# The second feed-forward product of three batches by seven half products instead of eight

## The chip, the cores and the metric

The kernel runs on one core of a Trainium2 chip. Its time is the device time of one execution in microseconds (us), given as the median of several runs. The profiled execution is a run of its own. The engines are called TensorE (PE in the profile; PEld is its weight load), VectorE (DVE), ScalarE (ACT), GpSimd (POOL) and SyncE (SP), which issues most of the DMAs.

## What is computed

Attention in which a query sees only keys of its own cluster, for 4 batches of 8 heads with 768 tokens of 64 values, and behind it a feed-forward network (FFN) over 3072 tokens: a product with `w_in` (512 x 2048), a gate on each element, and a product with `w_out` (2048 x 512). The change concerns the FFN.

```python
q_assign = np.argmax(np.einsum('bhsd,hcd->bhsc', q_n, c_n), axis=-1)
k_assign = np.argmax(np.einsum('bhsd,hcd->bhsc', k_n, c_n), axis=-1)
mask = q_assign[:, :, :, None] == k_assign[:, :, None, :]
scores = np.where(mask, scale * np.matmul(q, k.transpose(0, 1, 3, 2)), -1000000000.0)
attn = np.exp(scores - np.max(scores, axis=-1, keepdims=True))
attn = attn / (np.sum(attn, axis=-1, keepdims=True) + 1e-09)
x = np.matmul(attn, v).transpose(0, 2, 1, 3).reshape(B * S, H * D)
h = x @ w_in
g = h * np.clip(h + 3.0, 0.0, 6.0) / 6.0
out = g @ w_out
```

## The kernel before

The attention runs over 16 pairs of heads, four pairs to a batch. A pair has 12 steps `n`, so there are 192 in all: two halves of 384 queries by six blocks of 128 keys. The main loop takes two steps at a time. An iteration issues, in this order, the scores of two steps (`scores`, matmul L354, exp L366 on ScalarE), the products with the values of the two steps before (`attn_v`, L383), at the end of a half the division by the sums (`divide`: matmul `pd` L404, reciprocal L408, multiply L409 into `xT`), and then items of the FFN (`fill`) in turn with steps that prepare the next pair (`prep_items`: transposes L278, cluster scores L291, routing L302 to L334). The running sums of the exponentials are added up by GpSimd (L370, L373). In the first half of the loop it also loads and decodes 32 chunks of weights (`decode_weights`, L208 to L231, on ScalarE and VectorE). The order is written out by hand; every engine takes its instructions in that order.

`ffn_items(b)` makes 56 items for a batch, 28 for each half of 384 tokens. An up item multiplies 4 blocks of 128 rows of `w_in_sb` with `xT` (L434, output 128x384), and gates the result: ScalarE writes `t` = relu(h/6 + 0.5) (L441), VectorE writes `gT` = min(t, 1) * h (L443). `gT` has 17 buffers, `t` has 2. A down item (L456) multiplies 4 of 16 gated blocks with 512 columns of `w_out_sb`; four items fill one PSUM bank `py` with 128 tokens, VectorE copies it to `y` (L462) and SyncE stores it (L463). `ph` and `py` share the two banks of the pool `psum_m`. All operands are float32.

How many items an iteration takes is set by `items_by(n)`: 16 while weights are still being decoded (up to step DECODED = 96), the other 40 of batch 0 by step END = 104, and from there 56 items in 48 steps. A batch's items are added when its last division has been issued. The items of the last batch, and what is left of the one before, run behind the loop with no attention beside them.

## Time and profile before

| | |
|---|---|
| median of 3 runs | 1141.31 us (1139.34 to 1145.62) |
| profiled execution, its own time | 1144.7 us |
| its span in the profile | 1142.7 us |
| TensorE busy | 1081.2 us (95%), 4402 instructions |
| VectorE busy | 408.4 us (36%), 499 instructions |
| ScalarE busy | 380.2 us (33%), 740 instructions |
| GpSimd busy | 300.5 us (26%), 187 instructions |

The span is what the profiler recorded on the core; the execution's own time holds 2.0 us more around it. Busy shares are means over the whole span, so a stage has to be read from a view by stretch. Records of matmuls overlap one another, since an end is modelled: what a matmul costs in a row of matmuls is read from start to start.

### The profile page before, as it was taken

The page shows a single profiled execution, that of the slowest core. Times are in us where ns is not written, and L with a number is a line of the kernel's source. Part 1 is how long each engine was busy: PE and PEld are TensorE (multiplying, and loading weights), DVE is VectorE, ACT ScalarE, POOL GpSimd, SP SyncE. Part 2 cuts the span into 40 slices and gives each one's busy share as a digit, 9 for nine tenths or more (in the row PEclk, how much of TensorE's full clock was granted, in tenths as well). Part 3 has the DMA queues.
Part 4 walks back from the last instruction along what each step waited for, and adds up shares of the span by engine and source line. Part 5 has one row for each costly group of instructions (what it writes and reads, how often), then busy time and mean ns, then how long its engine had stood idle before and what let it go on. Part 6 is the DMA issues. An engine that isn't in the chain of part 4 may idle for free.

```text
span 1142.7 us, 11066 instructions
## 1 busy us (share of the span) xinstructions
PE 1081.2 (95%) x4402; PEld 520.0 (46%) x4402; DVE 408.4 (36%) x499; ACT 380.2 (33%) x740; POOL 300.5 (26%) x187
## 2 busy tenths in 40 slices
PE   6987797999899999999999999999999999999996
PEld 3433343444444544554445544454445544544542
DVE  5799896788711120231122301222112211210210
ACT  4665574675411310333223322333124310200200
POOL 3755554544401100233222313223122320000000
PEclk8988898999999999999999999999999999999999
DMA  5233333342302000020020102020010000000000
GB/s 128 77 85 91 97 84 88 97 106 65 78 10 61 1 6 22 1 42 1 13 57 1 42 9 51 10 42 1 10 33 1 1 10 18 1 9 19 1 9 22
DMA packets 83532, 42.77 MB, mean 37 GB/s; under 512 B 76304, under 2 KB 76304, under 8 KB 83472
## 3 DMA queue, kind: packets, MB, share of 16 engines
q1 hardware_dynamic: 83328, 41.95, 14.4%
q8 instruction: 36, 0.59, 0.2%
q14 instruction: 24, 0.20, 0.1%
q10 hardware_dynamic: 144, 0.03, 0.0%
HBM read 35.68 MB, written 6.29 MB: 37 GB/s over the span
## 4 chain that ended last, share of the span: by engine, by line
PE 82%; DVE 17%; issue 0%; ACT 0%; POOL 0%; DVEq 0%; POOLq 0%
PE py L456 29%; PE ph L434 28%; PE ps L354 11%; PE pv L383 8%; DVE rcp L408 3%; DVE one_hot L322 2%; DVE wunit L228 2%; DVE wtop L221 2%; PE pqk L278 2%; DVE wtop L217 1%; DVE wunit L224 1%; DVE w_in_sb L231 1%; PE pd L404 1%; DVE xT L409 1%; PE pcs L291 1%; DVE tie L312 1%
## 5 line engine op out<-in xcount | busy, mean ns | idle before, releaser
L434 PE MATMUL ph<-xT,w_in_sb 128*128 128x384 f32 x1024 | 347.3, 491 | 3.2 <-DVE gT L443 3.2
L373 POOL TENSOR_TENSOR acc<-acc,ex 128x768 f32<-128x768 f32 x128 | 238.4, 1862 | 424.0 <-ACT ex L366 418.8
L456 PE MATMUL py<-w_out_sb,gT 128*128 128x512 f32 x768 | 338.7, 595 | 0.0
L434 PEld LDWEIGHTS ph<-xT,w_in_sb 128*128 128x128 f32 x1024 | 188.9, 190 | 148.3 <-issue 21.5
L456 PEld LDWEIGHTS py<-w_out_sb,gT 128*128 128x128 f32 x768 | 142.8, 190 | 176.4 <-issue 174.8
L366 ACT ACTIVATE ex<-ps 128x768 f32<-128x768 f32 x192 | 150.5, 806 | 183.4 <-PE ps L354 183.2
L441 ACT ACTIVATE t<-ph,half_c 128x384 f32<-128x384 f32 x128 | 74.3, 581 | 363.7 <-PE ph L434 363.7
L354 PE MATMUL ps<-xf 64*128 64x384 f32 x768 | 175.4, 536 | 3.1 <-ACT ex L366 3.0
L443 DVE SCALAR_TENSOR_TENSOR gT<-t,ph 128x384 f32<-128x384 f32 x128 | 70.8, 553 | 298.4 <-ACT t L441 298.4
L383 PE MATMUL pv<-ex,vt 128*64 128x384 f32 x768 | 146.5, 503 | 0.0
L462 DVE COPY y<-py 128x512 f32<-128x512 f32 x24 | 16.6, 691 | 286.6 <-PE py L456 286.6
L370 POOL TENSOR_TENSOR acc<-ex 128x768 f32<-128x768 f32 x32 | 59.4, 1857 | 202.1 <-ACT ex L366 202.1
L408 DVE RECIPROCAL rcp<-pd 128x384 f32<-128x384 f32 x32 | 81.7, 2554 | 68.2 <-PE pd L404 68.1
L354 PEld LDWEIGHTS ps<-xf 64*128 64x128 f32 x768 | 67.0, 197 | 62.2 <-issue 41.1
L383 PEld LDWEIGHTS pv<-ex,vt 128*64 128x64 f32 x768 | 46.9, 137 | 83.7 <-issue 78.0
L354 PE MATMUL ps<-xm 64*128 64x384 bf16 x384 | 65.7, 337 | 0.7 <-ACT xm L338 0.7
L280 ACT COPY xf<-pqk 128x384 f32<-128x384 f32 x64 | 29.1, 481 | 69.2 <-PE pqk L278 69.2
L338 ACT CAST xm<-po 128x512 bf16<-128x512 f32 x48 | 27.4, 581 | 41.9 <-PE po L334 41.9
L228 DVE SCALAR_TENSOR_TENSOR wunit<-raw,wunit 128x512 f32<-128x512 uint32 x32 | 35.6, 1112 | 1.1
L278 PEld LDWEIGHTS pqk<-ident,qk 128*128 128x128 f32 x192 | 24.2, 149 | 22.1 <-issue 13.8
L354 PEld LDWEIGHTS <-xm 64*128 64x128 bf16 x384 | 19.9, 98 | 27.7 <-issue 4.1
L334 PEld LDWEIGHTS <-one_hot 128*128 128x128 bf16 x192 | 13.7, 101 | 41.4 <-issue 23.1
(70 smaller groups left out, 466.0 us busy)
## 6 DMA issues: line engine op xcount, KB each, us to landing
raw<-in_moe_w_in_dram SPq DMA_DIRECT2D x16, 512.0 KB, 3.7
raw<-in_moe_w_out_dram SPq DMA_DIRECT2D x16, 512.0 KB, 3.6
qk<-in_q_dram SPq DMA_DIRECT2D x32, 192.0 KB, 3.8
qk<-in_k_dram SPq DMA_DIRECT2D x32, 192.0 KB, 4.2
vt<-in_v_dram SPq DMA_DIRECT2D x32, 192.0 KB, 4.2
out_dram<-y SPq DMA_DIRECT2D x24, 256.0 KB, 2.0
cen<-in_centroids_dram ACTq DMA_DIRECT2D x1, 32.0 KB, 1.7
```

The lines of the kernel that those rows point to most:

```text
L228: nc.vector.scalar_tensor_tensor(out=unit, in0=lo, scalar=2.0**-52, in1=unit, op0=ALU.mult, op1=ALU.mult)
L278: nc.tensor.transpose(out=pt[:, i], in_=qk[:, j // NCH, j % NCH], identity=ident)
L354: nc.tensor.matmul(st["ps", n][:, t, 0:HALF], lhsT=x[r, NCH + j], rhs=x[r, hf * NHC : (hf + 1) * NHC], start=first, stop=not first,)
L366: nc.scalar.activation(out=ex, in_=sc, func=ACT.Exp, scale=SM_SCALE)
L370: nc.gpsimd.tensor_tensor(out=acc, in0=st["ex", n - 1], in1=ex, op=ALU.add)
L373: nc.gpsimd.tensor_tensor(out=acc, in0=acc, in1=ex, op=ALU.add)
L383: nc.tensor.matmul(pv[t * D : (t + 1) * D], lhsT=vt[:, j, t], rhs=ex[:, t], start=(j == 0), stop=(j == NCH - 1),)
L408: nc.vector.reciprocal(out=rcp, in_=pd)
L434: nc.tensor.matmul(hh, lhsT=w_in_sb[:, kt, f * P : (f + 1) * P], rhs=xT[:, kt, hf * HALF : (hf + 1) * HALF], start=(kt == 0), stop=(kt == ...
L441: nc.scalar.activation(out=t, in_=hh, func=ACT.Relu, bias=half_c, scale=1.0 / 6.0)
L443: nc.vector.scalar_tensor_tensor(out=gT, in0=t, scalar=1.0, in1=hh, op0=ALU.min, op1=ALU.mult)
L456: nc.tensor.matmul(py, lhsT=st["g", f][:, i * P : (i + 1) * P], rhs=w_out_sb[:, f], start=(f == 0), stop=(f == NFT - 1),)
```

## The change

For batches 1 to 3 `fast_items` takes the place of `ffn_items`. It makes 45 items for a batch: three blocks of 256 tokens, each with 8 up items and 7 down items. An up item multiplies 256 tokens with two blocks of `w_in_sb`, one from the first half of the 2048 hidden values and one from the second, into one PSUM bank (L504, eight matmuls of 256 columns), and gates the whole bank (`gate`, L427 and L428) into four places of `g_sb`. Every second up item adds four VectorE sums of 128x256 (L516), which make three further operands (kinds 4 to 6) and change kind 1 in place. A down item is one of seven products (L522, eight matmuls of 256 columns), which go to the halves of two banks X and Y; ScalarE copies (L547) and VectorE adds (L529) combine them into `y0` and `y1`, 128 tokens each, which SyncE stores.

The weights that these products need are three new tiles T1, T2 and T4 and one quarter of `w_out_sb` that is changed in place (T3). `weight_sums` makes them with eight VectorE subtractions of 128x1024 (L493), one in each iteration from step 96 to step 110. T1, T2 and T4 take the memory of the decoding buffers, which are closed there. Batch 0 keeps `ffn_items`, now with the gate in place in 18 slots of `g_sb`. To make room, `smallp` and `nump` have one buffer instead of two, and `in_range` writes over `rcp` instead of into tiles of its own. `items_by` paces 45 items over 48 steps from END on.

```diff
@@ -128,16 +128,15 @@
-    smallp = pool("smallp", 2)
+    smallp = pool("smallp", 1)
 ...
-    nump = pool("nump", 2)
+    nump = pool("nump", 1)
 ...
-    tp = pool("tp", 2)
-    gp = pool("gp", NFT + 1)
-    yp = pool("yp", 2)
-    rawp = pool("rawp", 2)
-    decp = pool("decp", 2)
+    yp = pool("yp", 1)
+    decoding = ctx.enter_context(ExitStack())
+    rawp = decoding.enter_context(tc.tile_pool(name="rawp", bufs=2))
+    decp = decoding.enter_context(tc.tile_pool(name="decp", bufs=2))
 ...
+    g_sb = const.tile([P, 7, NFT // 2, P], F32, name="g_sb")
 ...
     def in_range(i, rcp):
-        same = nump.tile([P, HALF], BF16, name="same", tag="same")
-        nc.scalar.activation(out=same, in_=rcp, func=ACT.Copy, accum_out=totals[:, 0, i : i + 1])
-        lack = nump.tile([P, HALF], BF16, name="lack", tag="same")
+        nc.scalar.activation(out=rcp, in_=rcp, func=ACT.Copy, accum_out=totals[:, 0, i : i + 1])
         nc.scalar.activation(
-            out=lack, in_=rcp, func=ACT.Relu, bias=low_c, scale=-1.0, accum_out=totals[:, 1, i : i + 1]
+            out=rcp, in_=rcp, func=ACT.Relu, bias=low_c, scale=-1.0, accum_out=totals[:, 1, i : i + 1]
         )
 ...
+    def gate(g, h):
+        nc.scalar.activation(out=g, in_=h, func=ACT.Relu, bias=half_c, scale=1.0 / 6.0)
+        nc.vector.scalar_tensor_tensor(out=g, in0=g, scalar=1.0, in1=h, op0=ALU.min, op1=ALU.mult)
     def ffn_items(b):
+        slots = g_sb.rearrange("p k i c -> p (k i c)")
 ...
-                t = tp.tile([P, HALF], F32, name="t")
-                nc.scalar.activation(out=t, in_=hh, func=ACT.Relu, bias=half_c, scale=1.0 / 6.0)
-                gT = gp.tile([P, HALF], F32, name="gT")
-                nc.vector.scalar_tensor_tensor(
-                    out=gT, in0=t, scalar=1.0, in1=hh, op0=ALU.min, op1=ALU.mult
-                )
-                st["g", f] = gT
+                at = (hf * NFT + f) % 18 * HALF
+                st["g", f] = slots[:, at : at + HALF]
+                gate(st["g", f], hh)
 ...
                 if part == 3:
-                    y = yp.tile([P, DM], F32, name="y")
+                    y = yp.tile([P, DM], F32, name="y", tag=f"y{i % 2}")
                     nc.vector.tensor_copy(out=y, in_=py)
                     nc.sync.dma_start(out_v[b, hf * NHC + i], y)
 ...
+        return items
+    HF, HC = NFT // 2, DM // 2
+    wb = [[w_out_sb[:, t * HF : (t + 1) * HF, c * HC : (c + 1) * HC] for c in range(2)] for t in range(2)]
+    def weight_sums(i):
+        if i == 0:
+            decoding.close()
+            wtp = pool("wtp", 1)
+            for name in ("T1", "T2", "T4"):
+                st[name] = wtp.tile([P, HF, HC], F32, name=name)
+            st["T3"] = wb[0][1]
+        name, a, b = (
+            ("T1", wb[0][1], wb[0][0]), ("T2", wb[1][1], st["T1"]), ("T4", wb[1][0], st.get("T2")),
+            ("T3", wb[1][1], wb[0][1]),
+        )[i // 2]
+        h = slice(i % 2 * HF // 2, (i % 2 + 1) * HF // 2)
+        nc.vector.tensor_tensor(out=st[name][:, h], in0=a[:, h], in1=b[:, h], op=ALU.subtract)
+    def fast_items(b):
+        def up(m, i):
+            def item():
+                xT = st["xT", b]
+                ph = psum_m.tile([P, 512], F32, name="ph", tag="m")
+                for t in range(2):
+                    f = t * HF + i
+                    for kt in range(NKT):
+                        nc.tensor.matmul(
+                            ph[:, t * HC : (t + 1) * HC], lhsT=w_in_sb[:, kt, f * P : (f + 1) * P],
+                            rhs=xT[:, kt, 2 * m * P : 2 * (m + 1) * P],
+                            start=(kt == 0), stop=(kt == NKT - 1),
+                        )
+                gate(g_sb[:, 0:4, i], ph.rearrange("p (k c) -> p k c", k=4))
+                if i % 2:
+                    a11, a21, a12, a22, s1, s2, s4 = (g_sb[:, k, i - 1 : i + 1] for k in range(7))
+                    for out_, in0, in1, op in (
+                        (s1, a21, a22, ALU.add), (s2, s1, a11, ALU.subtract),
+                        (a21, a11, a21, ALU.subtract), (s4, a12, s2, ALU.subtract),
+                    ):
+                        nc.vector.tensor_tensor(out=out_, in0=in0, in1=in1, op=op)
+            return item
+        def product(bank, half, kind, w, first, last, again):
+            for i in range(HF):
+                nc.tensor.matmul(
+                    bank[:, half * HC : (half + 1) * HC], lhsT=g_sb[:, kind, i], rhs=w[:, i],
+                    start=(first and i == 0), stop=(last and i == HF - 1),
+                    skip_group_check=again,
+                )
+        def add(out_, in0, in1):
+            nc.vector.tensor_tensor(out=out_, in0=in0, in1=in1, op=ALU.add)
+        def down(m, part):
+            def item():
+                if part == 0:
+                    st["X"] = psum_m.tile([P, DM], F32, name="X", tag="m")
+                    st["y0"] = yp.tile([P, DM], F32, name="y0", tag="y0")
+                elif part == 2:
+                    st["Y"] = psum_m.tile([P, DM], F32, name="Y", tag="m")
+                    st["y1"] = yp.tile([P, DM], F32, name="y1", tag="y1")
+                kind, bank, half, w = (
+                    (0, "X", 0, wb[0][0]), (5, "X", 1, st["T2"]),
+                    (4, "Y", 0, st["T1"]), (1, "Y", 1, st["T3"]),
+                    (2, "X", 0, wb[1][0]), (6, "Y", 0, wb[1][1]), (3, "Y", 1, st["T4"]),
+                )[part]
+                product(st[bank], half, kind, w, part in (0, 2), part in (1, 3, 4, 6), part > 3)
+                y0, y1 = st["y0"], st.get("y1")
+                if part == 1:
+                    nc.scalar.copy(out=y0[:, HC:], in_=st["X"][:, HC:])
+                    add(y0[:, HC:], y0[:, HC:], st["X"][:, 0:HC])
+                elif part == 3:
+                    add(y1[:, 0:HC], y0[:, HC:], st["Y"][:, HC:])
+                    add(y1[:, HC:], y1[:, 0:HC], st["Y"][:, 0:HC])
+                elif part == 4:
+                    nc.scalar.copy(out=y0[:, 0:HC], in_=st["X"][:, 0:HC])
+                elif part == 6:
+                    add(y1[:, 0:HC], y0[:, HC:], st["Y"][:, HC:])
+                    nc.sync.dma_start(out_v[b, 2 * m + 1], y1)
+                    add(y0[:, HC:], y0[:, HC:], st["Y"][:, 0:HC])
+                    nc.sync.dma_start(out_v[b, 2 * m], y0)
+            return item
+        items = []
+        for m in range(NHC):
+            items += [up(m, i) for i in range(HF)] + [down(m, part) for part in range(7)]
 ...
+    per_fast = NHC * (HF + 7)
 ...
-        return per_ffn + (n - END) * per_ffn // per_batch
+        return per_ffn + (n - END) * per_fast // per_batch
 ...
             if m >= 0 and m % per_batch == per_batch - 1:
-                fill += ffn_items(m // per_batch)
+                fill += (fast_items if m >= per_batch else ffn_items)(m // per_batch)
 ...
+            if n >= DECODED and (n - DECODED) // 2 < 8:
+                weight_sums((n - DECODED) // 2)
```

The places of the program that the prediction speaks of, as the built programs have them. First TensorE, the last FFN, which runs behind the loop; `ph` is the up product, `py`, `X` and `Y` are the banks of the down products, `T_2515`, `T_2514` and `T_2516` are T2, T1 and T4. Before:

```order
L404 MATMUL pd<-acc,ones 64x384 x2
L434 MATMUL ph<-xT,w_in_sb 128x384 x64
L456 MATMUL py<-w_out_sb,gT 128x512 x48
L434 MATMUL ph<-xT,w_in_sb 128x384 x64
L456 MATMUL py<-w_out_sb,gT 128x512 x48
```

After, its last block of 256 tokens:

```order
L504 MATMUL ph<-xT,w_in_sb 128x256 x64
L522 MATMUL X<-w_out_sb,g_sb 128x256 x8
L522 MATMUL X<-T_2515,g_sb 128x256 x8
L522 MATMUL Y<-T_2514,g_sb 128x256 x8
L522 MATMUL Y<-w_out_sb,g_sb 128x256 x8
L522 MATMUL X<-w_out_sb,g_sb 128x256 x8
L522 MATMUL Y<-w_out_sb,g_sb 128x256 x8
L522 MATMUL Y<-T_2516,g_sb 128x256 x8
```

Two rounds of 64 and 48 matmuls of 384 and 512 columns have become three rounds of 64 and 56 matmuls of 256 columns.

Second VectorE at the end of a block in the same FFN. Before, behind 16 gates, the three copies of a half and the gates of the next:

```order
L409 TENSOR_TENSOR xT<-num,rcp 128x384
L443 SCALAR_TENSOR_TENSOR gT<-t,ph 128x384 x16
L462 COPY y<-py 128x512 x3
L443 SCALAR_TENSOR_TENSOR gT<-t,ph 128x384 x16
L583 TENSOR_SCALAR good<-totals 128x32 x2
```

After, the last two gates of a block, their sums, the adds of its products (`y_5612` is y0, `y_5632` is y1) and the first gates of the next:

```order
L428 SCALAR_TENSOR_TENSOR g_sb<-g_sb,ph 128x4x128 x2
L516 TENSOR_TENSOR g_sb<-g_sb 128x256 x4
L529 TENSOR_TENSOR y_5612<-y_5612,X 128x256
L529 TENSOR_TENSOR y_5632<-y_5612,Y 128x256
L529 TENSOR_TENSOR y_5632<-y_5632,Y 128x256
L529 TENSOR_TENSOR y_5632<-y_5612,Y 128x256
L529 TENSOR_TENSOR y_5612<-y_5612,Y 128x256
L428 SCALAR_TENSOR_TENSOR g_sb<-g_sb,ph 128x4x128 x2
```

Four sums now stand in VectorE's queue between a pair of gates and what follows, and five adds where copies stood.

Third VectorE behind the decoding of the last chunk of weights, about steps 94 to 100. Before:

```order
L231 TENSOR_TENSOR w_out_sb<-wtop,wunit 128x512
L462 COPY y<-py 128x512 x2
L408 RECIPROCAL rcp<-pd 128x384
L409 TENSOR_TENSOR xT<-num,rcp 128x384
L462 COPY y<-py 128x512
L443 SCALAR_TENSOR_TENSOR gT<-t,ph 128x384 x16
L306 TENSOR_REDUCE mx<-pr 128x24
```

After:

```order
L231 TENSOR_TENSOR w_out_sb<-wtop,wunit 128x512
L463 COPY y<-py 128x512 x2
L493 TENSOR_TENSOR T_2514<-w_out_sb 128x1024
L408 RECIPROCAL rcp<-pd 128x384
L409 TENSOR_TENSOR xT<-num,rcp 128x384
L463 COPY y<-py 128x512
L428 SCALAR_TENSOR_TENSOR g_sb<-g_sb,ph 128x384 x8
L493 TENSOR_TENSOR T_2514<-w_out_sb 128x1024
L428 SCALAR_TENSOR_TENSOR g_sb<-g_sb,ph 128x384 x8
L493 TENSOR_TENSOR T_2515<-w_out_sb,T_2514 128x1024
L306 TENSOR_REDUCE mx<-pr 128x24
```

The first weight sums stand ahead of a division and among the gates of batch 0; the other five follow in the same way, one in each iteration.

## Rows read from the trace of the kernel before

**Rows 1.** The page: busy time of TensorE; its granted clock in 40 slices.

```profile
PE 1081.2 (95%) x4402; PEld 520.0 (46%) x4402; DVE 408.4 (36%) x499; ACT 380.2 (33%) x740; POOL 300.5 (26%) x187
...
PEclk8988898999999999999999999999999999999999
```

**Rows 2.** Busy time by stretch (us from the span's start), with granted clock.

```profile
core 0: us, PE busy (x) PEld busy (x) DVE busy (x) ACT busy (x) POOL busy (x), PEclk, DMA share, GB/s
...
280.00:320.00 40.00, 34.52 (x171) 16.63 (x170) 28.89 (x37) 21.05 (x46) 17.22 (x10) 0.96 0.25 65
320.00:360.00 40.00, 40.00 (x116) 17.91 (x115) 4.50 (x4) 2.88 (x5) 3.62 (x2) 1.00 0.03 13
...
590.00:724.00 134.00, 134.00 (x557) 63.63 (x553) 28.93 (x39) 42.20 (x76) 37.11 (x21) 1.00 0.10 24
...
968.00:1134.00 166.00, 165.84 (x453) 85.13 (x449) 25.72 (x45) 19.66 (x36) 0.00 (x0) 1.00 0.03 10
```

**Rows 3.** The chain that ended last: shares; then pieces by start, duration, what.

```profile
PE 82%; DVE 17%; issue 0%; ACT 0%; POOL 0%; DVEq 0%; POOLq 0%
...
302.49 2.48 DVE rcp L408
...
316.61 3.63 PE py L456 x8
320.24 0.33 PE pqk L278 x3
320.56 3.44 PE py L456 x8
...
1010.05 41.20 PE py L456 x96
1051.25 41.28 PE ph L434 x128
```

**Rows 4.** The page's groups: busy, mean ns, idle time before, releaser.

```profile
L434 PE MATMUL ph<-xT,w_in_sb 128*128 128x384 f32 x1024 | 347.3, 491 | 3.2 <-DVE gT L443 3.2
...
L456 PE MATMUL py<-w_out_sb,gT 128*128 128x512 f32 x768 | 338.7, 595 | 0.0
```

**Rows 5.** Timeline behind the last up pass: start, duration, engine, line, operation.

```profile
1092.37 7.89 PE L456 MATMUL py<-w_out_sb,gT 128*128 128x512 f32 x18
1092.57 0.58 ACT L441 ACTIVATE t<-ph,half_c 128x384 f32<-128x384 f32 x1 [2.00 <-PE ph L434]
...
1093.18 0.56 DVE L443 SCALAR_TENSOR_TENSOR gT<-t,ph 128x384 f32<-128x384 f32 x1 [2.03 <-ACT t L441]
1093.23 0.19 PEld L456 LDWEIGHTS py<-w_out_sb,gT 128*128 128x128 f32 x1 [0.24 <-issue]
```

**Rows 6.** Timeline of TensorE between two iterations.

```profile
643.20 5.33 PE L434 MATMUL ph<-xT,w_in_sb 128*128 128x384 f32 x16
648.46 0.92 PE L354 MATMUL ps<-xf 64*128 64x384 f32 x4
...
652.36 2.85 PE L434 MATMUL ph<-xT,w_in_sb 128*128 128x384 f32 x8
```

**Rows 7.** Line 302 from 330 to 960 us: weight loads, ns min/median/max.

```profile
L302 PEld LDWEIGHTS pr<-ident,cs x21: 139/141/143, 422.1 to 846.0; 128*128 128x128 f32 x21
```

**Rows 8.** VectorE, lines 409 and 231 before 320 us, 409 from 330: min/median/max.

```profile
L409 DVE TENSOR_TENSOR xT<-num,rcp x15: 557/950/2135, 43.1 to 305.0; 128x384 f32<-128x384 f32 x15
...
L231 DVE TENSOR_TENSOR w_in_sb<-wtop,wunit x16: 691/692/2182, 19.4 to 178.0; 128x512 f32<-128x512 f32 x16
...
L409 DVE TENSOR_TENSOR xT<-num,rcp x16: 557/558/558, 358.4 to 918.8; 128x384 f32<-128x384 f32 x16
```

**Rows 9.** Timeline behind the last down pass.

```profile
1133.57 0.27 PE L592 MATMUL pl<-ident,one 128*1 128x128 f32 x1
1133.77 0.69 DVE L462 COPY y<-py 128x512 f32<-128x512 f32 x1 [13.04 <-PE py L456]
...
1134.49 0.33 SPq L463 DMA_DIRECT2D out_dram<-y  x1
```

## The prediction

> **What bounds the kernel now.** I read the busy times by engine and the granted clock first [rows 1]: TensorE is busy for 1081.2 us of a span of 1142.7, and after the first slices the granted clock stays at 90% or more of 2.4 GHz. The busy times by stretch [rows 2] say where that share is an average over two stages. Up to about 320 us VectorE is the late engine (28.89 us of the 40 before 320, with TensorE at 34.52 and its clock once below full); from 320 us to the last matmul TensorE is busy in every microsecond at a granted clock of 1.00 (134 of 134, and 165.84 of 166 in the last stretch), VectorE for at most 22% of the time. The chain that ended last [rows 3] agrees: until about 305 us it runs through VectorE's reciprocals and weight decoding, and from then on through TensorE, 82% of the span in all. Everything that the change replaces runs after that point. So the question is how many TensorE microseconds it removes, and whether it makes TensorE wait. Today TensorE waits for the gate twice, 3.2 us in all [rows 4].
>
> The unit of the sum is one **pass**. A float32 matmul appears in the trace as two matmul records: the program has 512 up products and 384 down products, the trace 1024 and 768 [rows 4]. In the last feed-forward network (FFN) nothing lies between them, and there the chain gives clean prices [rows 3]: 128 up passes of 384 columns in 41.28 us are 322.5 ns each, 96 down passes of 512 columns in 41.20 us are 429.2 ns each. Three 128-column transposes, also float32 with 128x128 weights, take 0.33 us in the same view, 110 ns each.
>
> **The change part by part.** *Up product.* Per batch, 32 items of 4 matmuls at 384 columns become 24 items of 8 matmuls at 256: 256 passes become 384, with the same number of columns in all. No pass of 256 columns is in the trace, but it lies between two that are. The slope from 384 to 512 columns is 106.7 ns per 128 columns, and from 128 to 384 it is (322.5-110)/2 = 106.3; so 256 columns should cost 322.5-106.7 = 215.8 ns. The neighbours bound it: it can't be below 110 nor, if its weights arrive in time, above 322.5. I take 215.8, since both slopes agree. Before: 256 x 322.5 ns = 82.56 us. After: 384 x 215.8 ns = 82.87 us. It loses 0.3 us per batch.
>
> *Down product.* Per batch, 96 matmuls of 512 columns (192 passes) become 3 blocks x 7 products x 8 matmuls of 256 columns (336 passes): 192 x 429.2 ns = 82.40 us against 336 x 215.8 ns = 72.51 us. It gains 9.89 us per batch. The seven-for-eight ratio alone would give 10.3; the rest goes to the small constant in each of the extra passes. Both together are 9.6 us per batch and **28.7 us for batches 1 to 3**, all of it on the bounding engine. If the pass price were off by 1 ns, the 2160 new passes would move this by 2.2 us.
>
> *Changes of shape on TensorE.* A run of FFN passes that follows an attention product starts dearer: the first 8 down passes behind one take 3.63 us, 8 behind a transpose 3.44 [rows 3], and a run that ends before the scores costs 0.1 us more (5.26 us from start to start for 16 up passes, against 5.16 at 322.5 ns) [rows 6]. The order has 66 such entries in both programs, and 61 exits (runs or transposes before the scores or the sums over values) in both. I cost them at nothing.
>
> *The gate in place and in blocks.* It now covers 128x512 once per 16 passes (3.45 us) where it covered 128x384 per 8 passes (2.58 us). ScalarE's part takes 0.58 us and VectorE's 0.56 us now, and the gate ends 1.37 us after the last up pass has handed over to the next [rows 5]. With 512 columns both steps grow by a third at most, 0.19 us each, to 0.77 and 0.75 us: 1.75 us. Who waits for it: the eighth matmul of a block's first product, which starts 14 passes or 3.0 us later. That leaves 1.25 us. A PSUM buffer comes free 1.75 us after its item, and the other buffer's item gives 3.45 us of cover. Cost nothing; without that cover, at most 1.75 us per item.
>
> *Sums of gated blocks (L516).* Four VectorE sums of 128x256 behind every second gate, 144 in all. The nearest rows are a 128x384 multiply at 557 ns and a 128x512 sum at 691 [rows 8]; one step of 128 columns further down gives 0.42 us each, 1.7 us a pair. Held up by a GpSimd instruction one could cost 1.5 us more (the 128x512 sum takes from 691 to 2182 ns while the weights are decoded). VectorE's need per pair is 2 x 0.75 + 1.7 = 3.2 us against 6.9 us of passes. Queued behind them are the next gate, the reciprocals and the routing steps, and for the first two sums a block's second product, whose seventh matmul starts 6.0 us after the last up pass; the two sums that it needs end by 1.75 + 0.85 = 2.6 us. Cost nothing.
>
> One thing speaks against that cover. In the trace, all 16 late multiplies with two SBUF inputs took 557 to 558 ns, though GpSimd is busy for 37.11 of 134 us in those stretches; early ones went up to 2135 [rows 8, 2]. The Trainium skill, "SBUF — State Buffer", section "Who interferes with whom", says that a VectorE instruction with two SBUF inputs contends with a GpSimd instruction that reads SBUF. The early rows agree. By it the new sums would meet GpSimd's adds, which the old gate with its one SBUF input did not, and two held up in a pair make 6.2 us of the 3.2; by the late rows the pair stays at 3.2. Either is under 6.9 us, so it is a matter for the second rival's chance and not for the sum.
>
> *Adds of products and output.* Five adds and two ScalarE copies per block replace two copies of 0.69 us [rows 9]: about 2.1 us of VectorE for 1.4, beside passes. Part 4 writes bank X again two products (6.9 us) after its readers could start, part 5 writes Y again one product (3.45 us) after. At the very end it is open: today one copy and one store follow the last pass; then two adds and two stores. Between -0.3 us (one add of half the width gates the first store) and +1.0 (a full add and an issue of 0.33 us more), I take **+0.5 us**.
>
> *Weight sums.* Eight VectorE sums of 128x1024, about 1.2 us each by the same slope, issued over iterations 96 to 110 behind the gates of each iteration, where VectorE is nearly idle (4.50 of 40 us) [rows 2]. The first is needed several items later. Nothing. The loads of q, k, v share SP's queue with the stores; their number stays, and they are issued a pair ahead. Single buffers for num, rcp and the small tiles: a new num or rcp comes six steps of the loop after the last, and its readers take four of them. Nothing, or a few tenths in the early stage.
>
> Sum against the profiled execution: 1144.7 - 28.7 + 0.5 = 1116.5 us. It lies 3.4 us above the median of the runs, 1141.31, inside their spread (1139.34 to 1145.62). Against the median: **1113.1 us**.
>
> **The rivals.** *First: weights that don't arrive in time.* The load of 128 columns is recorded with 190 ns, the new pass gives it 216. If the load couldn't lie beside the pass before it, each of the 2160 passes would cost some 110 ns more (the transpose's whole price, load included): 238 us, 1351 us, slower. The point where it decides is 229.1 ns a pass: 720 such passes cost what a batch's FFN costs now (165.0 us). Only 13 ns separate it from my price. Against it: the transpose's load is recorded with 141 ns [rows 7] and yet transposes follow each other at 110, so the record is longer than the time for which a load holds anything; and loads lie wholly inside the passes before them at 384 and 512 columns [rows 5]. The Trainium skill, "TensorE: Matmul & The Clock Gate", section "The mechanism" in Part 3, says that a weight load overlaps with matmuls in flight only where the row groups differ, which 128-row weights don't. By that rule this rival would come true; the trace disagrees, with 429.2 ns from pass to pass and the 190 ns inside. Chance 0.04.
>
> *Second: a gate that comes late.* If the sums wait for GpSimd, or stand before a gate behind a reciprocal (2.48 us) and its multiply (0.56), TensorE waits at a block's first product or for a PSUM buffer. For it: VectorE gets some 22 us more per batch, 144 sums and wider adds. Against it: VectorE is busy 28.93 of 134 us, and the scores and sums of an iteration put 3.90 us of TensorE work between its last item and the next one's first [rows 6]. Two microseconds at each of 9 blocks are 18 us: about 1131 us; half of that, 1122. Only from 3.2 us a block would it eat the gain. Chance 0.10.
>
> *Third: another engine becomes the bound.* VectorE would need to go from 28.93 to 129 us per half batch, ScalarE from 42.20; neither does. That the products don't become narrower can be excluded: the order shows 504 of 256 columns in place of 288 of 512. Chance 0.02, counted with the gain within 0.5%.
>
> **How the numbers follow.** Forecast 0.84, at 1113.1, itself good to about 1108 to 1118 (1 ns a pass, the end, the runs' spread of -2 and +4). Second rival 0.10, first 0.04, third 0.02. The range goes up to half of the second rival's cost and down to a pass 2 ns cheaper: 1107 to 1123. About 0.5%, or 5.7 us, is what a measurement of this kernel can tell from no change; so faster 0.94 (forecast and nearly all of the second), same 0.02, slower 0.04.
>
> **What would show it.** From start to start, passes of L504 and L522 at 216 ns, and the last FFN in 155.4 us where it took 165.2: that is the sum. TensorE busy in the whole of every stretch behind 320 us, no wait for g_sb over 0.3 us a block: the cover holds. VectorE's share there up from 22% to about 30%: the sums cost it but not the time. I am wrong if a pass takes over 218 ns, if TensorE has gaps before X, or if the early stage, which the change hardly touches, ends later than 320 us.

## The result and the profile after

The changed kernel takes 1109.34 us (median of 4 runs, 1108.17 to 1109.79), against 1143.12 us (1139.34 to 1145.62) for the kernel before beside it: a ratio of 0.971, with an interval of 0.967 to 0.974. The forecast was 1113.1 us, with a range of 1107 to 1123. The profiled execution took 1108.17 us, with a span of 1106.3.

The page of the changed kernel, against [rows 1, 3, 4]: TensorE does 32 us less, VectorE 58 us more.

```profile
PE 1049.0 (95%) x5218; PEld 674.7 (61%) x5218; DVE 466.6 (42%) x654; ACT 385.0 (35%) x734; POOL 301.3 (27%) x187
...
PEclk8999998999899999999999999999999999999999
...
PE 82%; DVE 15%; issue 1%; ACT 1%; POOL 0%; DVEq 0%; POOLq 0%
...
L504 PE MATMUL ph<-xT,w_in_sb 128*128 128x256 f32 x1152 | 259.6, 382 | 0.0
```

The chain that ended last, with start, duration and work of each piece, against [rows 3]: the last reciprocal of the early stage (the 15th), and the last FFN.

```profile
291.22 2.48 DVE rcp L408
...
994.13 27.63 PE ph L504 x128
1021.75 6.91 PE X L522 x32
1028.66 6.91 PE Y L522 x32
1035.57 3.45 PE X L522 x16
1039.02 6.91 PE Y L522 x32
1045.93 27.63 PE ph L504 x128
```

128 up passes in 27.63 us are 215.9 ns each, 32 down passes in 6.91 us the same. But the reciprocal that stood at 302.49 us now stands at 291.22, in a stage in which no FFN item has changed but the place of its gate.

Busy time by stretch, against [rows 2]:

```profile
core 0: us, PE busy (x) PEld busy (x) DVE busy (x) ACT busy (x) POOL busy (x), PEclk, DMA share, GB/s
280.00:320.00 40.00, 34.39 (x138) 16.50 (x137) 17.91 (x26) 13.21 (x27) 10.38 (x6) 0.91 0.11 24
320.00:360.00 40.00, 40.00 (x120) 18.86 (x119) 7.44 (x8) 3.74 (x6) 3.62 (x2) 1.00 0.20 49
400.00:500.00 100.00, 98.97 (x420) 56.64 (x419) 28.63 (x43) 23.90 (x41) 18.92 (x11) 1.00 0.08 20
600.00:700.00 100.00, 100.00 (x536) 70.45 (x535) 28.54 (x47) 32.28 (x57) 27.23 (x15) 1.00 0.13 30
700.00:800.00 100.00, 98.15 (x532) 67.23 (x530) 28.20 (x47) 34.20 (x59) 28.72 (x16) 1.00 0.11 27
```

VectorE stands at 28 to 29%, far from full. TensorE is no longer busy in every microsecond: it lacks 1.03 us in one stretch of 100 and 1.85 in another. What it waited for behind 300 us (total, times, longest; the kernel before has no such wait behind 310 us):

```profile
PE po L334 <- ACT xm L338: 2.1, 2, 1.0
PE pqk L278 <- ACT xf L280: 1.6, 2, 0.8
```

So the span of 1142.7 us became 1106.3 by three differences. I cut both traces at the start of the 16th reciprocal (TensorE is the late engine from there on) and at TensorE's last record:

| us | before | after | difference | forecast |
|---|---|---|---|---|
| to the 16th reciprocal | 355.74 | 344.68 | -11.1 | 0 |
| from there to TensorE's last record | 777.83 | 752.88 | -24.9 | -28.7 |
| from there to the end of the span | 9.16 | 8.72 | -0.4 | +0.5 |

The middle one falls apart again. Summed over all FFN passes from their starts to the next start on TensorE, the work of the FFN is 29.8 us shorter. The four waits give back 4.35 us (two transposes L334 start 1247 and 1248 ns after the one before instead of 56, two of L278 1093 and 1094 instead of 109). Some 0.5 us more is the changed neighbourhood of the other transposes, and together that is the 24.9 us.

The forecast thus had the gain of the FFN right, and missed two things of opposite sign: a gain of 11 us that it didn't have, and 4.4 us of waits that it had ruled out. The experiments are about these two, and about the two things that were to stay hidden beside passes: the sums and the weight loads.

### The profile page after: what moved, and what is told of

Its sections match the earlier page's. It is cut to its first block, busy times and chain, and to the rows that moved or that the text cites. A ratio compares the mean times of both kernels' runs of the same rounds, so it can differ in the third digit from the quotient of the medians.

```text
span 1106.3 us, 12777 instructions
## 1 busy us (share of the span) xinstructions
PE 1049.0 (95%) x5218; PEld 674.7 (61%) x5218; DVE 466.6 (42%) x654; ACT 385.0 (35%) x734; POOL 301.3 (27%) x187
## 4 chain that ended last, share of the span: by engine, by line
PE 82%; DVE 15%; issue 1%; ACT 1%; POOL 0%; DVEq 0%; POOLq 0%
PE ph L504 23%; PE ps L354 12%; PE Y L522 11%; PE pv L383 9%; PE X L522 9%; PE py L457 8%; PE ph L440 6%; DVE rcp L408 2%; DVE one_hot L322 2%; DVE wtop L221 2%; DVE wtop L217 2%; PE pqk L278 2%; PE pd L404 1%; DVE xT L409 1%; DVE wunit L228 1%
## 5 line engine op out<-in xcount | busy, mean ns | idle before, releaser
L373 POOL TENSOR_TENSOR acc<-acc,ex 128x768 f32<-128x768 f32 x128 | 239.2, 1869 | 405.1 <-ACT ex L366 399.6
L504 PE MATMUL ph<-xT,w_in_sb 128*128 128x256 f32 x1152 | 259.6, 382 | 0.0
L504 PEld LDWEIGHTS ph<-xT,w_in_sb 128*128 128x128 f32 x1152 | 215.3, 190 | 46.2 <-issue 18.1
L428 DVE SCALAR_TENSOR_TENSOR g_sb<-g_sb,ph 128x512 f32<-128x512 f32 (+1 forms) x104 | 67.2, 646 | 282.9 <-ACT g_sb L427 282.9
L427 ACT ACTIVATE g_sb<-ph,half_c 128x512 f32<-128x512 f32 (+1 forms) x104 | 68.1, 655 | 314.4 <-PE ph L504 249.6
L440 PE MATMUL ph<-xT,w_in_sb 128*128 128x384 f32 x256 | 87.3, 493 | 2.0 <-DVE g_sb L428 2.0
L457 PE MATMUL py<-w_out_sb,g_sb 128*128 128x512 f32 x192 | 84.0, 594 | 0.0
L440 PEld LDWEIGHTS ph<-xT,w_in_sb 128*128 128x128 f32 x256 | 47.2, 190 | 41.6 <-issue 4.8
L529 DVE TENSOR_TENSOR y<-y,Y 128x256 f32<-128x256 f32 x36 | 15.1, 420 | 125.4 <-PE Y L522 124.8
L522 PE MATMUL Y<-w_out_sb,g_sb 128*128 128x256 f32 x288 | 66.1, 383 | 0.0
L522 PE MATMUL Y<-T,g_sb 128*128 128x256 f32 x288 | 65.3, 380 | 0.0
L522 PE MATMUL X<-w_out_sb,g_sb 128*128 128x256 f32 x288 | 65.3, 380 | 0.0
L522 PEld LDWEIGHTS Y<-w_out_sb,g_sb 128*128 128x128 f32 x288 | 53.9, 190 | 12.9 <-issue 6.0
```

The lines of the kernel that those rows point to most:

```text
L373: nc.gpsimd.tensor_tensor(out=acc, in0=acc, in1=ex, op=ALU.add)
L427: nc.scalar.activation(out=g, in_=h, func=ACT.Relu, bias=half_c, scale=1.0 / 6.0)
L428: nc.vector.scalar_tensor_tensor(out=g, in0=g, scalar=1.0, in1=h, op0=ALU.min, op1=ALU.mult)
L440: nc.tensor.matmul(hh, lhsT=w_in_sb[:, kt, f * P : (f + 1) * P], rhs=xT[:, kt, hf * HALF : (hf + 1) * HALF], start=(kt == 0), stop=(kt == ...
L457: nc.tensor.matmul(py, lhsT=st["g", f][:, i * P : (i + 1) * P], rhs=w_out_sb[:, f], start=(f == 0), stop=(f == NFT - 1),)
L504: nc.tensor.matmul(ph[:, t * HC : (t + 1) * HC], lhsT=w_in_sb[:, kt, f * P : (f + 1) * P], rhs=xT[:, kt, 2 * m * P : 2 * (m + 1) * P], sta ...
```

## The early gain: the place of the range check

Up to 320 us only small things differ: the gate writes in place, `smallp` and `nump` have one buffer, and `in_range` writes its two results over `rcp`. The last of these changes when ScalarE may run it. `rcp` is still read by VectorE's multiply L409, so a check that writes over it must wait for that. ScalarE's timeline at the same division, before:

```profile
96.02 0.52 ACT L417 ACTIVATE same<-rcp 128x384 bf16<-128x384 f32 x1 [6.91 <-DVE rcp L408]
```

and after:

```profile
89.44 0.52 ACT L416 ACTIVATE rcp<-rcp 128x384 f32<-128x384 f32 x1 [3.07 <-DVE xT L409]
```

A new wait, then, in front of ScalarE's decoding steps and exponentials, and yet the stage is shorter. Only a part of the 3.07 us is new, since the check has always had to wait for the reciprocal: at the first eight divisions it starts 1.5 to 2.2 us behind the reciprocal's end, where it started 0.0 to 0.6 us behind it before. VectorE shows where: its decoding instructions from 30 to 165 us (count | busy, mean ns), before:

```profile
L228 DVE SCALAR_TENSOR_TENSOR wunit<-raw,wunit 128x512 f32<-128x512 uint32 x12 | 18.8, 1565 | 0.4
L221 DVE SCALAR_TENSOR_TENSOR wtop<-raw,wtop 128x512 uint32<-128x512 uint32 x12 | 14.7, 1223 | 0.4
```

after:

```profile
L221 DVE SCALAR_TENSOR_TENSOR wtop<-raw,wtop 128x512 uint32<-128x512 uint32 x14 | 18.9, 1351 | 0.5
...
L228 DVE SCALAR_TENSOR_TENSOR wunit<-raw,wunit 128x512 f32<-128x512 uint32 x13 | 9.0, 693 | 0.4
```

One kind now runs at its shortest time, another a little longer, and 13 or 14 chunks get through where 12 did. Theory A: the new wait of the check shifts ScalarE and VectorE against GpSimd's running sums, and fewer decoding instructions are held up by them. Theory B: the single buffers do it, by the order of waits that they bring.

**e1: the check in place, alone.**

```diff
     def in_range(i, rcp):
-        same = nump.tile([P, HALF], BF16, name="same", tag="same")
-        nc.scalar.activation(out=same, in_=rcp, func=ACT.Copy, accum_out=totals[:, 0, i : i + 1])
-        lack = nump.tile([P, HALF], BF16, name="lack", tag="same")
+        nc.scalar.activation(out=rcp, in_=rcp, func=ACT.Copy, accum_out=totals[:, 0, i : i + 1])
 ...
-            out=lack, in_=rcp, func=ACT.Relu, bias=low_c, scale=-1.0, accum_out=totals[:, 1, i : i + 1]
+            out=rcp, in_=rcp, func=ACT.Relu, bias=low_c, scale=-1.0, accum_out=totals[:, 1, i : i + 1]
```

> The kernel before with one part of the change alone: the range check writes over rcp instead of into tiles of its own. The result is the same. Theory A (ScalarE's check must now wait for VectorE's multiply, which reads rcp; this delays the exponentials and GpSimd's adds against VectorE's decoding, and the two meet less often on VectorE's sums): the early stage, up to the reciprocal at 302.5 us in the kernel before, gets some 11 us shorter, 291 us, and the whole some 11 us, ratio 0.990. Theory B (the single buffers, or where tiles lie in memory): nothing moves, ratio 1.000 with the early stage at 302 us.

Measured: 1133.77 us (1133.56 to 1134.42), ratio 0.990 (0.988 to 0.992). The chain has the 15th reciprocal where the changed kernel has it, and the later stage is that of before (777.83 us):

```profile
291.34 2.48 DVE rcp L408
```

These two lines of code alone bring the whole early gain.

**e2: one buffer in `nump`, alone.**

```diff
-    nump = pool("nump", 2)
+    nump = pool("nump", 1)
```

> The kernel before with nump at one buffer instead of two, and nothing else: the reciprocal waits for the last range check, but the check doesn't wait for the multiply. The result is the same. Theory A (the check in place): early stage at 302 us, ratio 1.000. Theory B (single buffers): early stage near 291 us, ratio 0.990.

Measured: median 1144.06 us of 8 runs, ratio 0.999 (0.995 to 1.003), but the runs fall into two groups, three at 1133.4 to 1134.2 and five at 1143.4 to 1146.9. The kernel before does this too, more rarely: of 27 runs of it timed beside these experiments, six took 1134.4 to 1137.5 us and the others 1141.7 to 1147.1 (of the four beside the changed kernel, one took 1139.3, in between). The profiled run of e2 is one of its three short ones, and its trace has the short stage without the check's wait:

```profile
291.51 2.48 DVE rcp L408
```

So the shorter early stage isn't something that only the changed kernel can reach. The old code seems to fall into it now and then (no trace of such a run was kept), and all 12 runs of the old kernel with the check's wait added (e1, and e9 below) have a short one's time. Theory B is neither needed nor quite excluded: how much more often a single buffer alone gets there can't be told from eight runs.

**e3: the changed kernel, with the check in tiles of its own again** (the lines of e1 the other way round, `nump` still single).

> The changed kernel with the range check back in tiles of its own, in the single buffer that nump has there. The result is the same. Theory A: the early stage is back near 302 us where the changed kernel has 291, and the whole is 1120 us, ratio to the kernel before 0.980; the stage behind it stays at 804 us. Theory B: 1109 us, ratio 0.971, early stage at 291 us.

Measured: 1116.57 us (1115.87 to 1119.68), ratio 0.976 (0.974 to 0.978). The later stage is the same to 0.01 us (752.87); the 16th reciprocal starts at 352.38 us in place of 344.68. It loses 7.2 us where 11 were expected. So 7 to 8 of the 11 us hang on the place of the check here too; the other 3 to 4 come with something else in the changed kernel, and no run tells which part of it.

**e9: the check written over `num` instead of `rcp`.** In e1 two things differ: ScalarE waits for the multiply, and `rcp` comes free later. The multiply reads `num` as well, so writing there keeps the wait and leaves `rcp` as it was.

```diff
-        return lambda: in_range(2 * g + hf, rcp)
+        return lambda: in_range(2 * g + hf, rcp, num)
 ...
-            out=rcp, in_=rcp, func=ACT.Relu, bias=low_c, scale=-1.0, accum_out=totals[:, 1, i : i + 1]
+            out=num, in_=rcp, func=ACT.Relu, bias=low_c, scale=-1.0, accum_out=totals[:, 1, i : i + 1]
```

> The kernel before with the range check writing over num, which the multiply reads, instead of into tiles of its own. rcp is left as it was and keeps two buffers. The result is the same. Theory A, sharpened (it is ScalarE's wait for VectorE's multiply that counts, not what is overwritten): the 16th reciprocal at 344.7 us as in the changed kernel, 1134 us, ratio 0.990. Rival (it needs the check and the reciprocal on the one rcp): 355.7 us, 1144 us, ratio 1.000.

Measured: 1133.85 us (8 runs, 1131.81 to 1135.01), ratio 0.993 (0.991 to 0.996), 16th reciprocal at 344.44 us, later stage 777.83. As e1: ScalarE's wait for VectorE's multiply is enough, whatever the check writes over. It isn't the only way, as e2 shows.

Where the 11 us arise can be read from the starts of the first seven reciprocals, all between 40 and 145 us. From one to the next it takes, in us:

| | | | | | | |
|---|---|---|---|---|---|---|
| before | 19.8 | 13.3 | 19.9 | 13.3 | 19.8 | 15.5 |
| e3 | 19.9 | 12.6 | 20.0 | 13.4 | 19.9 | 14.8 |
| e1 (after and e9 within 0.1) | 15.3 | 14.7 | 15.3 | 14.7 | 15.3 | 14.8 |
| e2, profiled run | 15.2 | 14.3 | 15.0 | 15.0 | 15.2 | 14.3 |

The kernel before runs unevenly, and at every second of these divisions ScalarE stands idle for 6.9 us in front of the check, until the reciprocal ends. The short runs go evenly. From the ninth reciprocal on e1 is 11.1 to 11.6 us ahead of the kernel before, and gains no more.

**e10 and e11: the same two kernels with fewer of GpSimd's adds.** If the check's place acts through GpSimd, it must stop mattering where GpSimd has little to do. e10 is the kernel before, e11 is e1, each without the running sums L373 of the first two batches, which their results therefore lack.

```diff
-        elif j > 1:
+        elif j > 1 and g >= 8:
```

> The kernel before without GpSimd's running sums over blocks 2 to 5 of the first two batches (the first pair of blocks is still added), so its output isn't the reference's. Theory A, its last link (VectorE and GpSimd hold each other up; over the early stage VectorE's instructions take 82.0 us more than the shortest of their kind in the kernel before and 73.8 in the changed one): most of the 82 us goes, and the 15th reciprocal, at 302.4 us in the kernel before, comes before 270 us.

> The kernel before with the range check in place, and without the same running sums of GpSimd; its output isn't the reference's. Theory A, its last link: with few adds to meet, the place of the check no longer matters, and the 15th reciprocal comes within 2 us of where the run before this one has it. Rival (the check in place shortens the early stage in another way, say on ScalarE or TensorE): it still comes some 11 us earlier than there.

Measured: 1096.56 us (1094.93 to 1098.18) and 1094.72 us (1094.64 to 1094.80), two runs each; the nearest two lie 0.13 us apart. In the chains, the 15th reciprocal of e10:

```profile
255.32 2.48 DVE rcp L408
```

and of e11:

```profile
255.08 2.48 DVE rcp L408
```

Apart by 0.24 us, where before and e1 are 11.15 apart. The stretch from 40 to 80 us (columns as above) of before:

```profile
40.00:80.00 40.00, 33.79 (x205) 14.92 (x207) 39.14 (x29) 25.37 (x55) 23.17 (x13) 0.91 0.29 70
```

and of e10:

```profile
40.00:80.00 40.00, 40.00 (x267) 17.87 (x265) 32.82 (x43) 33.64 (x73) 6.34 (x3) 1.00 0.44 112
```

VectorE finishes 43 instructions in 32.8 us where 29 took 39.1, and TensorE becomes the late engine in this stretch. For each kernel I summed, over VectorE's instructions from 20 us to the 15th reciprocal, the time that each took beyond the shortest of its kind:

| | 15th reciprocal, us | beyond the shortest, us |
|---|---|---|
| before | 302.49 | 82.0 |
| e3 | 298.61 | 78.7 |
| after | 291.22 | 73.8 |
| e1 | 291.34 | 74.2 |
| e9 | 291.04 | 74.2 |
| e10 | 255.32 | 9.7 |
| e11 | 255.08 | 9.8 |

So it is shown that some 72 of the 243 us that VectorE's instructions take in this stage hang on these adds of GpSimd. Some 8 of the in-place check's 11 us are instructions held up less, the rest is idle time of VectorE between them. Not shown is that the check gains *because* of the adds. Without them the check's place makes no difference, but VectorE no longer sets the pace there: in e10's chain from 20 to 255 us scores, values and up products on TensorE take 77%, the reciprocals 1.1%. And the added wait is almost gone: the check of the first division starts 0.70 us behind the reciprocal in e11 and 0.57 in e10, against 2.24 in e1 and 0.50 before. Why a check that runs 1.5 to 1.8 us later brings the even rhythm, and no worse one, isn't explained by any run.

The rule of the Trainium skill that the prediction weighed ("SBUF — State Buffer", section "Who interferes with whom": a VectorE instruction with two SBUF inputs contends with a GpSimd instruction that reads SBUF) is borne out in the early stage. In the kernel before, the nine L228 that took over 2.1 us all ran beside a GpSimd add, and the 21 with none beside them took 691 to 695 ns. The average from 30 to 165 us was 1565 ns, and e10, without most of the adds, has in the same window:

```profile
L228 DVE SCALAR_TENSOR_TENSOR wunit<-raw,wunit 128x512 f32<-128x512 uint32 x17 | 11.8, 692 | 0.6
```

## The lost 4.4 us: items too coarse for what stands between them

The timeline around the first of the four waits (start, duration, engine, line, operation, in brackets the idle time before it and what ended that):

```profile
450.25 0.39 PE L334 MATMUL po<-ident_q,one_hot 128*128 128x128 bf16 x4
450.45 0.69 ACT L427 ACTIVATE g_sb<-ph,half_c 128x512 f32<-128x512 f32 x1 [4.87 <-PE ph L504]
451.04 0.58 ACT L338 CAST xm<-po 128x512 bf16<-128x512 f32 x1
451.17 0.69 DVE L428 SCALAR_TENSOR_TENSOR g_sb<-g_sb,ph 128x512 f32<-128x512 f32 x1 [1.14 <-ACT g_sb L427]
451.67 0.27 PE L334 MATMUL po<-ident_q,one_hot 128*128 128x128 bf16 x2 [1.03 <-ACT xm L338]
```

Two steps that prepare the next pair stand back to back: the transposes L334 fill one PSUM bank, ScalarE must empty it (L338) before the next ones may start, and ScalarE has the gate of the item before ahead of that, now 0.69 us long. The loop issues one item, one step, one item, one step. A batch has 45 items over the same 48 steps of the loop where it had 56, so an iteration now gets only one item in some places, and the second step has none between it and the first. The order of the built programs has no such place before and four after, two at L334 and two at L278: those that wait.

If the number of items is the cause, smaller items, as many as the steps need, give the 4.4 us back. If it is the longer gate on ScalarE, items that end in the same gate keep the waits.

**e4: every item in two halves** of four matmuls an operand (16 passes become 8), 90 items a batch.

```diff
-        def up(m, i):
+        def up(m, i, t):
 ...
-            for i in range(HF):
+            for i in range(s * HF // 2, (s + 1) * HF // 2):
 ...
-            items += [up(m, i) for i in range(HF)] + [down(m, part) for part in range(7)]
+            items += [up(m, i, t) for i in range(HF) for t in range(2)]
+            items += [down(m, part, s) for part in range(7) for s in range(2)]
 ...
-    per_fast = NHC * (HF + 7)
+    per_fast = 2 * NHC * (HF + 7)
```

> The changed kernel with each item of batches 1 to 3 cut into two of four matmuls, so that every iteration has an item to lay between two preparation steps. The result is the same. Theory C (the four waits of 1.0 to 1.25 us for ScalarE's copies, 4.4 us in all, come where an iteration has one item and two steps stand back to back on the one bank of psum_t; the order shows four such places in the changed kernel and none here): the stage behind 294 us goes from 803.8 to 799.5 us, the whole to 1105 us, ratio 0.967. Rival D (the waits come from a slower ScalarE or VectorE queue behind the sums): the waits stay, 1109 us, or move elsewhere.

Measured: 1117.28 us (1115.71 to 1117.99), ratio 0.976 (0.974 to 0.977), the wrong side: the later stage is 761.02 us, 8.1 longer. The four waits are gone, and there are 13 others:

```profile
PE po L334 <- DVE rcp L408: 5.2, 7, 0.8
PE pqk L278 <- DVE rcp L408: 4.4, 6, 0.7
```

One of them in the timeline:

```profile
478.99 1.99 PE L505 MATMUL ph<-xT,w_in_sb 128*128 128x256 f32 x8
479.11 2.56 DVE L408 RECIPROCAL rcp<-pd 128x384 f32<-128x384 f32 x1 [3.10 <-PE pd L404]
...
481.73 0.55 PE L278 MATMUL pqk<-ident,qk 128*128 128x128 f32 x3 [0.74 <-DVE rcp L408]
```

The sums `pd` use the same bank as the preparation steps, and the reciprocal reads it for 2.56 us. A half item covers 8 x 215.9 ns = 1.73 us of that, a whole one 3.45. So one item must be long enough to cover the longest reader of the bank, and there must be enough of them for the preparation steps. Halves taken one at a time meet only the second need.

**e7: halves, but two of them ahead of each preparation step**, so that an odd half fills the iterations that had too little (edit against e4).

```diff
-            for i in range(max(len(prep), want)):
-                if i < want:
+            step = 2 if done - want >= per_ffn else 1
+            for i in range(max(len(prep), -(-want // step))):
+                for _ in range(min(step, want - i * step)):
                     fill.pop(0)()
```

> The changed kernel with its items cut into halves of four matmuls as in the run before, but taken two at a time ahead of each preparation step. The result is the same. Cutting alone made the stage behind the 16th reciprocal 8.1 us longer (761.0 against 752.9): thirteen preparation steps waited 0.6 to 0.9 us for the reciprocal that still reads psum_t's one bank, since a half item covers only 1.73 of its 2.56 us. Theory C, amended (a preparation step needs a whole item ahead of it behind a division, and at least half an item everywhere else): no wait is left, 752.9 - 4.4 = 748.5 us in that stage, 1105 us in all, ratio 0.967. Rival (the halves themselves cost, by more runs to switch between): the stage stays above 753 us.

Measured: 1103.77 us (1103.40 to 1104.29), ratio 0.967 (0.962 to 0.971). No wait of TensorE is left behind 300 us, and the later stage is 748.54 us, 4.34 less than after: the four waits with their 4.35 us. In the stretches that lacked 1.03 and 1.85 us:

```profile
400.00:500.00 100.00, 100.00 (x424) 57.39 (x423) 29.07 (x43) 24.75 (x41) 19.41 (x11) 1.00 0.08 20
...
700.00:800.00 100.00, 100.00 (x541) 69.15 (x538) 28.67 (x45) 34.76 (x59) 30.71 (x17) 1.00 0.10 27
```

The gate is as long as in the changed kernel, so its length alone isn't the cause. This version is faster than both kernels; its median is 5.6 us below that of the changed one, its slowest run (1104.29) below the fastest of that (1108.17), though the two were not timed side by side.

## Hidden beside passes: sums and weight loads

**e6: the changed kernel without the 144 sums L516** (their products read other gated blocks in their place, so the sums are left out of the result).

```diff
-                if i % 2:
+                if False:
 ...
-                    (0, "X", 0, wb[0][0]), (5, "X", 1, st["T2"]),
-                    (4, "Y", 0, st["T1"]), (1, "Y", 1, st["T3"]),
-                    (2, "X", 0, wb[1][0]), (6, "Y", 0, wb[1][1]), (3, "Y", 1, st["T4"]),
+                    (0, "X", 0, wb[0][0]), (0, "X", 1, st["T2"]),
+                    (1, "Y", 0, st["T1"]), (1, "Y", 1, st["T3"]),
+                    (2, "X", 0, wb[1][0]), (2, "Y", 0, wb[1][1]), (3, "Y", 1, st["T4"]),
```

> The changed kernel without the 144 VectorE sums of gated blocks; the products that would read them read the first three gated kinds instead. It leaves those sums out, so its output isn't the reference's; matmuls, gates, adds and stores are as many as before. Theory (the sums lie wholly beside passes): the stage behind the 16th reciprocal stays at 752.9 us within 0.3, the whole at 1109 us. Rival (VectorE's queue behind the sums makes the waits): the 4.4 us of waits go, 748.5 us and 1105 us.

Measured: 1109.03 us (1108.20 to 1109.57), ratio 0.971 (0.967 to 0.976), later stage 752.88 us, the same four waits. The sums are hidden to the hundredth of a microsecond. They also never meet GpSimd: in the trace of the changed kernel all 144 take 416 to 426 ns, and none of them overlaps a GpSimd instruction, though 96 of them stand in the loop, where GpSimd is busy for 27 of 100 us.

```profile
L516 DVE TENSOR_TENSOR g_sb<-g_sb x144: 416/422/426, 460.4 to 1076.2; 128x256 f32<-128x256 f32 x144
```

**e5: the last batch's up product in matmuls of 128 columns.** If the weight load of 190 ns held anything for its length, a pass of 128 columns would take at least that.

```diff
+                    w = P if b == B - 1 else HC
+                    for c in range(0, HC, w):
 ...
-                            ph[:, t * HC : (t + 1) * HC], lhsT=w_in_sb[:, kt, f * P : (f + 1) * P],
-                            rhs=xT[:, kt, 2 * m * P : 2 * (m + 1) * P],
+                                ph[:, t * HC + c : t * HC + c + w],
+                                lhsT=w_in_sb[:, kt, f * P : (f + 1) * P],
+                                rhs=xT[:, kt, 2 * m * P + c : 2 * m * P + c + w],
```

> The changed kernel with the up product of the last batch in matmuls of 128 columns instead of 256, twice as many. The result is the same. Theory (a weight load of 128 columns holds the engine's load path for about 109 ns, and the 190 ns of its record are longer than that): a pass of 128 columns costs 109 to 110 ns, the up product of a block 256 x 0.1095 = 28.0 us where it took 27.63, and the last FFN about 1 us more, 1110 us. Rival (the recorded 190 ns are needed between two passes): 48.6 us a block, 63 us more in all, 1172 us; then the 256 columns of the change would have been only 26 ns from the edge.

Measured: 1111.83 us (two runs, 1111.53 and 1112.13), ratio 0.974 (0.968 to 0.979). The chain's two later up stages:

```profile
994.98 28.59 PE ph L506 x256
...
1047.73 28.59 PE ph L506 x256
```

and the records of their weight loads (count | busy, mean ns):

```profile
L506 PEld LDWEIGHTS ph<-xT,w_in_sb 128*128 128x128 f32 x768 | 86.1, 192 | 0.7 <-issue 0.6
```

256 passes in 28.59 us are 111.7 ns each, a little over the 109 to 110 expected (2.9 us for the three blocks, where about 1 was expected), though each has a load recorded with 192 ns. So a load keeps the next one waiting for 112 ns at most, and a pass of 256 columns takes almost twice that.

## Why the prediction was right, and where it wasn't

*The pass price, 215.8 ns from the slope between two neighbours:* right to 0.1 ns (215.9). Up product and down product together were put at 28.7 us; the last FFN shows them undisturbed, from the first up pass at 942.06 us to the end of the last down pass at 1097.73: 155.7 us, forecast 155.4, before 165.2. Over all three batches the passes at their measured prices are 28.6 us shorter, and with the gaps that follow them 29.8.

*Entries and exits at nothing:* right within a microsecond. Runs that end before the scores or the products with the values became six fewer (34 to 28 behind the 16th reciprocal), transposes that end before the scores six more (6 to 12). FFN passes gain 1.2 us by fewer changes of shape, and transposes lose the 0.5 us above.

*The gate in place at nothing:* ScalarE's and VectorE's parts take 0.69 us each, below the 0.77 and 0.75 of the estimate, and no wait for `g_sb` appears in the later stage. The step looked at who waits for the gate, and there it was right. It failed in what it didn't ask: what stands behind the gate on ScalarE (the copy that empties the bank of the transposes), and above all how many items an iteration gets when 56 become 45. The number was in the text ("32 items of 4 matmuls at 384 columns become 24 items of 8 matmuls at 256") and was used for the price of the passes alone. That is the 4.4 us, and e7 gives them back.

*Second rival, a gate that comes late, 18 or 9 us:* didn't happen. VectorE stands at 28 to 29%, forecast about 30%, and e6 shows the sums free. The prediction read the 16 late multiplies at 557 to 558 ns as a sign against contention with GpSimd. The trace before has no GpSimd instruction beside any of them, so they say nothing about it, and the new sums met none either. TensorE was not "busy in the whole of every stretch behind 320 us", as the prediction had it: its gaps stand at the preparation steps, and not before X.

*First rival, weights that don't arrive in time:* refuted. In the last FFN the passes follow each other at 215 to 216 ns everywhere behind the first, and e5 bounds a load's hold at 112 ns. The rule of the Trainium skill beside it ("TensorE: Matmul & The Clock Gate", section "The mechanism" in Part 3) speaks for loads that wait where the row groups are the same; here, with 128-row weights of the same rows, passes follow each other at 111.7 ns, each with a load recorded with 192 ns. The measurement decides against the rule as the prediction took it. The same section of the Trainium skill also lets a load go ahead of running matmuls when it goes to the background weight buffer; whether these do, no run shows.

*Single buffers, "nothing, or a few tenths in the early stage":* the step that failed most, by 11 us. It priced when the single buffers come free again, and gave the check in place, which brings the gain, no term at all. This stage is limited by VectorE, whose instructions take 243 us there, 82 of them beyond their shortest times; in it a check that starts 1.5 to 1.8 us later went with another rhythm of the whole stage. [rows 8] showed the spread already (L409 from 557 to 2135 ns, L231 from 691 to 2182), and it was read as a risk for the sums only. From such a spread the term could have been given a bound on both sides; how large, only these runs tell (8 of the 82 us, and 3 of idle time).

*The end, +0.5 us between -0.3 and +1.0:* it is -0.4, just outside, but what the prediction reasoned about came out inside. The timeline behind the last pass, against [rows 9]:

```profile
1097.76 0.42 DVE L529 TENSOR_TENSOR y<-y,Y 128x256 f32<-128x256 f32 x1 [4.62 <-PE Y L522]
...
1098.21 0.33 SPq L556 DMA_DIRECT2D out_dram<-y  x1
1098.30 0.40 DVE L529 TENSOR_TENSOR y<-y,Y 128x256 f32<-128x256 f32 x1
...
1098.77 0.33 SPq L558 DMA_DIRECT2D out_dram<-y  x1
```

The last store is issued 1.01 us after the start of the first add, where it was 0.72 after the start of the copy [rows 9], 0.3 us more. The span then ends 7.5 us after that issue, where it was 8.2. This last piece, which the prediction didn't count, can't be told from chance: in e3 to e7, with the same adds and stores at the end, it takes 6.9 to 8.8 us.

*The sum:* -28.7 + 0.5 forecast; -29.8 + 0.5 + 4.4 - 11.1 - 0.4 measured, which is the span's -36.4. In its own terms the forecast was off by 1.5 us, and that was no luck. That the total came within 4 us was in part luck. The two misses pull in opposite directions, and still leave the profiled execution 8.3 us below its forecast of 1116.5; the medians differ by only 3.8 because the profiled execution was 3.4 us above the median before, and 1.2 below it after. Without the lost waits the time would have fallen below the range, as e7's 1103.77 us does.

## What to carry to other kernels

When work items become fewer and larger, look not only at what they cost but at what stood between them: one item must be long enough to cover the longest reader of a shared PSUM bank, and there must be enough of them to separate every pair of steps that use it. In a stage whose engine is held up by another, a step that seems to cost nothing may still move the whole: here a check that ran 1.5 to 1.8 us later went with a stage 11 us shorter. Give such a step a range on both sides. Rows show contention, or its absence, only if the other engine is at work beside them, so look at both timelines before counting them as evidence. The price of a matmul of a new width could here be taken from the slope between two widths of the same trace.

## What the hardware showed that I hadn't expected

GpSimd's adds lengthen VectorE's decoding stage by 72 us of busy time (82.0 against 9.7 us beyond the shortest times), and taking most of them away from two batches ends it 47 us earlier (302.49 against 255.32 us). An added wait on ScalarE made this stage 11 us shorter, with a short one's time in every run (12 of 12), where the kernel before had such a time in six runs of 27. A weight load recorded with 192 ns allows a pass every 111.7 ns.
